# Cutting the last 512 output columns of an attention and mixture-of-experts kernel into three pieces in place of two

## The chip, the cores and the metric

The kernel runs on one core of one Trainium2 chip. The metric is the device time of one execution in microseconds (us); less is better. A core has five engines that run side by side and wait for each other through semaphores: TensorE (matmuls, PE in the profile, with its weight loads shown as PEld), VectorE (DVE), ScalarE (ACT), GpSimd (POOL) and SyncE (SP, which issues most of the DMA transfers here). Matmuls write to PSUM, a small memory from which VectorE or ScalarE take the results into SBUF, and DMA engines bring those to the chip's main memory.

## What is computed

Two stages. Multi-query attention on a batch of 8, with 16 heads, 384 positions and a head size of 64 gives 3072 rows of 1024 numbers. Then each row goes to one of 16 experts (4 groups of 4), the one that two gates choose:

```python
# attention, per head: attn = softmax(q k^T / 8) ; x = attn v, rows of 16*64
for g in range(G):                       # 4 groups
    ...
    for e in range(Eg):                  # 4 experts in a group
        h = np.maximum(xg[mask_e] @ w1[g, e], 0.0)
        ye = h @ w2[g, e]
        out[tok_idx] = (g_w * e_w)[:, None] * ye     # cut: selection of rows
```

w1 and w2 are 1024 x 1024 for each expert. Nearly all rows of one batch element choose the same expert, and the kernel is built on that: for each batch element it computes the whole 384 rows with the expert chosen most often, weighs each row by its gate (zero for rows that chose another expert), and then adds the few remaining rows of one further batch element and expert in a compact form. Anything beyond that is done in a conditional block that normally isn't entered.

## The kernel before

The second product of each batch element is done in units: `st` is one of three blocks of 128 rows, `nh` one of two halves of 512 columns. `side` takes one of three PSUM buffers in turn. `P` is 128, `CW` 512, `FO` 8.

```python
def y_unit(st, nh):
    for i in range(parts(st, nh)):
        n = CW // parts(st, nh)
        cs = slice(nh * CW + i * n, nh * CW + (i + 1) * n)
        y = place(st, cs)
        ps = side([P, n], FP32, "yps")
        for fo in range(FO):
            nc.tensor.matmul(out=ps[:], lhsT=state["h"][:, fo, st * P:(st + 1) * P],   # L417
                             rhs=w2[:, fo, cs], start=(fo == 0), stop=(fo == FO - 1))
        if merge is None or not merge(st, cs, ps, y):
            nc.scalar.activation(out=y, in_=ps[:], func=ACTF.Copy, scale=gs_of()[:, st:st + 1])
        store(st, cs, y)
```

The closing unit is the second half (`nh == 1`) of the last row block of the last batch element. It is the last one to run. There, the remaining rows are merged in: `spread` puts them in their places with four small matmuls into two PSUM buffers (`lo` in a buffer of its own, `lo2` in one of the three), VectorE adds the first half to the row that is ready, and ScalarE copies the second half to SBUF (`yl`). Each piece of the closing unit is then scaled by the gate and added to its part of `yl` in one VectorE operation, and stored with a transfer of its own.

```python
def store(st, cs, y):
    if closes(st):
        if cs.start == 0:
            leftover["row"] = y
        else:
            nc.sync.dma_start(out=outv[b, :, st, cs], in_=y)                 # L445
    elif cs.stop == Dm:
        nc.sync.dma_start(out=outv[b, :, st, :], in_=rows[st][:])            # L447

def merge(st, cs, ps, y):
    if not closes(st) or cs.start == 0:
        return False
    if cs.start == CW:
        spread()
    nc.vector.scalar_tensor_tensor(out=y, in0=ps[:], scalar=gsel[b][:, st:st + 1],      # L454
        in1=leftover["y"][:, cs.start - CW:cs.stop - CW], op0=OP.mult, op1=OP.add)
    return True
# the closing unit has two parts, every other unit one:
return moe_units(..., lambda st, nh: 2 if closes(st) and nh == 1 else 1)

def spread():
    lo = [ps_m.tile([P, 2, CW], FP32, tag="o", name="lo"), side([P, 2, CW], FP32, "lo2")]
    for i in range(2):
        for c in (i, 2 + i):
            nc.tensor.matmul(out=lo[c // 2][:, c % 2, 0:QW], ...)            # L463
    row = leftover["row"]
    nc.vector.tensor_add(out=row..., in0=row..., in1=lo[0][:, :, 0:QW])      # L465
    nc.sync.dma_start(out=outv[B - 1, :, ST - 1, 0:CW], in_=row)             # L466
    t = pool.tile([P, CW], FP32, tag="pt", bufs=9, name="yl")
    nc.scalar.copy(out=t[:]..., in_=lo[1][:, :, 0:QW])                       # L468
    leftover["y"] = t
```

After the closing unit comes the condition of the rare block. Every engine loads the flag `rarei` from SBUF and branches on it:

```python
fill(1)                                            # runs the closing unit
nc.vector.tensor_scalar(out=raref[:, 0:1], ...)    # L754
nc.vector.tensor_scalar(out=raref[:, 1:2], ...)    # L755
nc.vector.tensor_add(out=rarei[:], in0=raref[:, 0:1], in1=raref[:, 1:2])     # L757
rare = nc.values_load(rarei[0:1, 0:1], ...)        # L758
# cut: functions used in the block only
rare_block = tc.If(rare > 0, preferred_fallthrough_block=False)              # its end is L810
with rare_block:
    ...                                            # a long block, not entered here
```

Of the kernel before, what the change touches and what calls it, by code (L numbers as in the profile page):

```python
# [13 lines left out]
P = 128  # L14
# [7 lines left out]
def kernel(  # L22
# [25 lines left out]
    CW = 512  # L48
# [27 lines left out]
    def side(shape, dtype, name):  # L76
        return ps_s.tile(shape, dtype, tag="s", name=name)

    q_raw, k_raw, v_sb, kT, qT, pt, xT, xbf, gsel, wts = {}, {}, {}, {}, {}, {}, {}, {}, {}, {}
# [315 lines left out]
        nc.vector.reduce_sum(out=gs[:], in_=gm[:], axis=AX)  # L395
        gsel[b] = gs

    def moe_units(w1, w2, xb, gs_of, place, store, merge=None, parts=lambda st, nh: 1):
        units = []
        state = {}  # L400

        def h_unit(fc):
            if fc == 0:
                state["h"] = pool.tile([P, FO, S], BF16, tag="hT", bufs=1, name="hT")
            ps = side([P, CW], FP32, "hps")
            for ko in range(KO):
                nc.tensor.matmul(out=ps[:, 0:S], lhsT=w1[:, ko, fc * P:(fc + 1) * P], rhs=xb[:, ko, :], start=(ko == 0), stop=(ko == KO - 1))  # L407
            nc.scalar.activation(out=state["h"][:, fc, :], in_=ps[:, 0:S], func=ACTF.Relu)  # L408

        def y_unit(st, nh):  # L410
            for i in range(parts(st, nh)):
                n = CW // parts(st, nh)
                cs = slice(nh * CW + i * n, nh * CW + (i + 1) * n)
                y = place(st, cs)
                ps = side([P, n], FP32, "yps")
                for fo in range(FO):
                    nc.tensor.matmul(out=ps[:], lhsT=state["h"][:, fo, st * P:(st + 1) * P], rhs=w2[:, fo, cs], start=(fo == 0), stop=(fo == FO - 1))  # L417
# [4 lines that stand above are left out]
        for fc in range(FO):  # L422
            units.append(lambda fc=fc: h_unit(fc))
        for st in range(ST):
            for nh in range(2):
                units.append(lambda st=st, nh=nh: y_unit(st, nh))
        return units

    def first_units(b):
        rows = {}  # L430

        def place(st, cs):
            if cs.start == 0:
                rows[st] = pool.tile([P, Dm], FP32, tag="y", bufs=3, name="y")
            return rows[st][:, cs]

        def closes(st):
            return b == B - 1 and st == ST - 1
# [14 lines that stand above are left out]
                spread()  # L453
            nc.vector.scalar_tensor_tensor(out=y, in0=ps[:], scalar=gsel[b][:, st:st + 1], in1=leftover["y"][:, cs.start - CW:cs.stop - CW], op0=OP.mult, op1=OP.add)  # L454
            return True
        return moe_units(wts[b][0], wts[b][1], xbf[b], lambda: gsel[b], place, store, merge, lambda st, nh: 2 if closes(st) and nh == 1 else 1)

    def spread():
        lo = [ps_m.tile([P, 2, CW], FP32, tag="o", name="lo"), side([P, 2, CW], FP32, "lo2")]
        for i in range(2):  # L460
            for c in (i, 2 + i):
                r = slice(CAP * c, CAP * c + CAP)
                nc.tensor.matmul(out=lo[c // 2][:, c % 2, 0:QW], lhsT=leftover["spread"][r, :], rhs=leftover["yc"][r, :], start=True, stop=True, tile_position=(CAP * c, 0))  # L463
        row = leftover["row"]
        nc.vector.tensor_add(out=row.rearrange("p (c n) -> p c n", c=2), in0=row.rearrange("p (c n) -> p c n", c=2), in1=lo[0][:, :, 0:QW])  # L465
        nc.sync.dma_start(out=outv[B - 1, :, ST - 1, 0:CW], in_=row)  # L466
        t = pool.tile([P, CW], FP32, tag="pt", bufs=9, name="yl")
        nc.scalar.copy(out=t[:].rearrange("p (c n) -> p c n", c=2), in_=lo[1][:, :, 0:QW])  # L468
        leftover["y"] = t
# [13 lines left out]
    def fill(n):  # L483
        while n > 0:
            if not units:
                if begun[0] >= B or begun[0] not in wts:
                    return
                units.extend(first_units(begun[0]))
                begun[0] += 1
            units.pop(0)()  # L490
            n -= 1
            ran[0] += 1
            if ran[0] == (FO + 2 * ST) * (B - 2) + FO:
                leftover_w1()
            if ran[0] == (FO + 2 * ST) * (B - 1):
                leftover_w2()
# [87 lines left out]
    for p in range(NP):  # L584
        b, st = divmod(p, ST)
# [49 lines left out]
        if p in PHASES:  # L635
            n = PHASES[p]
# [135 lines left out]
    def pair_units(b_reg, w1, w2, xe, ge):  # L772
        acc = pool.tile([P, ST, Dm], FP32, tag="xT", bufs=1, name="acc")

        def store(st, cs, y):
            if st == ST - 1 and cs.stop == Dm:
                nc.gpsimd.dma_start(out=outv[bass.ds(b_reg, 1)].rearrange("a p s d -> (a p) s d"), in_=acc[:], accum_op=OP.add, max_dma_last_dim=4096)
        return moe_units(w1, w2, xe, lambda: ge, lambda st, cs: acc[:, st, cs], store)
# [31 lines left out]
    with rare_block:  # L810
# [7 lines left out]
      with tc.If(ok < 1):  # L818
# [4 lines left out]
          with tc.For_i(0, B * H, 1) as i:  # L823
# [13 lines left out]
              for qt in range(ST):  # L837
# [5 lines left out]
                  at = pool.tile([P, S], FP32, tag="presum", bufs=1, name="at")  # L843
# [62 lines left out]
```

## Time and profile before

| | before |
|---|---|
| time, median of three runs | 460.92 us (460.87 to 461.02) |
| span of the profiled execution | 459.6 us |
| TensorE busy | 449.4 us, 98% |
| VectorE busy | 308.4 us, 67% |
| ScalarE busy | 242.0 us, 53% |
| closing unit, first piece's matmuls begin | 449.66 us |
| last compute operation (L757) begins | 453.08 us |

The span is the time from the first to the last instruction of one profiled execution. Times in the timeline and in the chain of work are counted from its start. In a line of the timeline stand the start, the duration, the engine, the line of the kernel and the operation with its output and inputs; in brackets, idle time of the engine ahead of it and what ended it. "x8" says that eight instructions are merged in the line. A name with a q (SPq, PEldq) is the instruction queue of an engine: waits, branches, register loads and the issue of transfers, which don't count as work.

### The profile page before, as it was taken

The page shows a single profiled execution, that of the slowest core. Times are in us where ns is not written, and L with a number is a line of the kernel's source. Part 1 is how long each engine was busy: PE and PEld are TensorE (multiplying, and loading weights), DVE is VectorE, ACT ScalarE, POOL GpSimd, SP SyncE. Part 2 cuts the span into 40 slices and gives each one's busy share as a digit, 9 for nine tenths or more (in the row PEclk, how much of TensorE's full clock was granted, in tenths as well). Part 3 has the DMA queues.
Part 4 walks back from the last instruction along what each step waited for, and adds up shares of the span by engine and source line. Part 5 has one row for each costly group of instructions (what it writes and reads, how often), then busy time and mean ns, then how long its engine had stood idle before and what let it go on. Part 6 is the DMA issues. An engine that isn't in the chain of part 4 may idle for free.

```text
span 459.6 us, 10200 instructions
## 1 busy us (share of the span) xinstructions
PE 449.4 (98%) x4208; PEld 199.8 (43%) x4208; DVE 308.4 (67%) x488; ACT 242.0 (53%) x345; POOL 60.5 (13%) x83
## 2 busy tenths in 40 slices
PE   8999999999999999999999999999999999999893
PEld 6343445333643345433553335433454335434552
DVE  3899965499717996099843997269960999574411
ACT  2966643676337753576346773376535764542331
POOL 1004003000120113000030001200130000500000
PEclk9999999999999999999999999999999999999997
DMA  8787997996699395992979747994869910799982
GB/s 154 99 146 109 218 208 120 258 201 139 107 177 254 74 189 96 235 224 74 157 113 266 140 118 124 167 258 80 170 102 233 234 69 11 115 211 245 274 212 104
DMA packets 152454, 74.55 MB, mean 162 GB/s; under 512 B 120256, under 2 KB 138944, under 8 KB 152400
## 3 DMA queue, kind: packets, MB, share of 16 engines
q0 software_dynamic: 28416, 37.81, 48.4%
q1 hardware_dynamic: 122656, 35.68, 33.3%
q8 instruction: 35, 0.57, 0.5%
q10 hardware_dynamic: 1328, 0.33, 0.4%
q14 instruction: 19, 0.16, 0.1%
HBM read 92.62 MB, written 19.01 MB: 243 GB/s over the span
## 4 chain that ended last, share of the span: by engine, by line
PE 89%; DMA 4%; issue 2%; DVE 1%; POOL 0%; ACT 0%; ACTq 0%; SPq 0%; POOLq 0%
PE s L251 28%; PE o L290 25%; PE hps L407 16%; PE yps L417 16%; PE gps L312 2%; DMA x_bf<-xbf 2%; DMA xe<-x_bf 2%; DMA qn<-in_q_dram 1%; PE qps L228 1%; POOL xbf L301 0%; DVE presum L261 0%; PE sm L273 0%; PE pb L715 0%; DVE rinv L280 0%; DVE xT L300 0%
## 5 line engine op out<-in xcount | busy, mean ns | idle before, releaser
L253 ACT ACTIVATE pt<-s 128x1024 f32<-128x1024 f32 x144 | 142.1, 1026 | 72.3 <-PE s L251 71.5
L251 PE MATMUL s<-qT,kT 64*64 64x512 f32 x1152 | 142.7, 594 | 0.0
L290 PE MATMUL o<-pt,v 64*64 64x512 f32 x1152 | 141.1, 590 | 0.0
L261 DVE TENSOR_TENSOR presum<-presum,pt 128x1024 f32<-128x1024 f32 x96 | 116.6, 1215 | 15.2 <-ACT pt L253 9.8
L407 PE MATMUL hps<-xbf,w 128*128 128x384 bf16 x512 | 86.7, 326 | 0.0
L417 PE MATMUL yps<-w,hT 128*128 128x512 bf16 (+1 forms) x392 | 85.7, 375 | 0.0
L259 DVE TENSOR_TENSOR presum<-pt 128x1024 f32<-128x1024 f32 x24 | 29.4, 1223 | 76.8 <-ACT pt L253 75.4
L290 PEld LDWEIGHTS o<-pt,v 64*64 64x64 f32 x1152 | 43.4, 133 | 76.8 <-issue 73.0
L251 PEld LDWEIGHTS s<-qT,kT 64*64 64x64 f32 x1152 | 40.8, 133 | 66.8 <-issue 60.0
L301 POOL CAST xbf<-xT 128x1024 bf16<-128x1024 f32 x24 | 25.0, 1043 | 302.8 <-DVE xT L300 302.8
L407 PEld LDWEIGHTS <-w 128*128 128x128 bf16 x512 | 48.2, 98 | 37.6 <-issue 6.5
L419 ACT ACTIVATE y<-yps,gsel 128x512 f32<-128x512 f32 x47 | 32.3, 688 | 58.8 <-PE yps L417 57.2
L408 ACT ACTIVATE hT<-hps 128x384 bf16<-128x384 f32 x64 | 31.3, 489 | 52.1 <-PE hps L407 48.0
L417 PEld LDWEIGHTS <-hT 128*128 128x128 bf16 x392 | 37.6, 98 | 44.1 <-issue 2.4
L145 POOL DMA_DIRECT2D w<-in_moe_w_dram x36 | 24.8, 708 | 58.2 <-DVE gsel L395 45.0
L300 DVE TENSOR_TENSOR xT<-o,rinv 128x1024 f32<-128x1024 f32 x24 | 29.2, 1215 | 2.5 <-PE o L290 2.5
L280 DVE STREAM_TRANSPOSE rinv<-rc 128x1024 f32<-128x1024 f32 x24 | 29.9, 1246 | 0.8
L265 DVE TRANSPOSE_TENSOR_REDUCE fold<-presum 128x32 f32<-128x1024 f32 x24 | 29.6, 1232 | 0.0
L243 DVE STREAM_TRANSPOSE qT<-qraw 128x1024 f32<-128x1024 f32 x20 | 23.6, 1202 | 0.0
L209 ACT ACTIVATE qraw<-qraw 128x1024 f32<-128x1024 f32 x21 | 22.0, 1048 | 0.0
L273 PEld LDWEIGHTS sm<-fold,sel 64*64 64x64 f32 x192 | 7.3, 133 | 13.3 <-issue 13.3
L371 ACT ACTIVATE ex<-dl 128x60 f32<-128x60 f32 x8 | 2.0, 253 | 20.1 <-DVE dl L369 20.1
(152 smaller groups left out, 162.0 us busy)
## 6 DMA issues: line engine op xcount, KB each, us to landing
w<-in_moe_w_dram POOLq DMA_DIRECT2D x36, 512.0 KB, 11.5
w<-in_moe_w_dram POOLq DMA_DIRECT2D x9, 2048.0 KB, 26.0
out_dram<-y SPq DMA_DIRECT2D x23, 512.0 KB, 6.9
qraw<-in_q_dram SPq DMA_DIRECT2D x56, 192.0 KB, 3.7
x_bf<-xbf SPq DMA_DIRECT2D x8, 768.0 KB, 3.9
v<-in_v_dram SPq DMA_DIRECT2D x16, 96.0 KB, 3.1
k<-in_k_dram SPq DMA_DIRECT2D x28, 48.0 KB, 2.7
qn<-in_q_dram SPq DMA_DIRECT2D x4, 256.0 KB, 5.2
```

The costliest lines, as they stand in the source:

```text
L251: nc.tensor.matmul(out=ps[64 * c:64 * c + 64, a, :], lhsT=kT[b][r, j * D:(j + 1) * D], rhs=qT[p][r, c * CW:(c + 1) * CW], start=True, stop ...
L253: nc.scalar.activation(out=t[:], in_=ps[:], func=ACTF.Exp, scale=scale)
L259: nc.vector.tensor_add(out=presum[p][:], in0=pt[p, 0][:], in1=pt[p, 1][:])
L261: nc.vector.tensor_add(out=presum[p][:], in0=presum[p][:], in1=pt[p, j][:])
L265: nc.vector.tensor_reduce(out=fold[p][:], in_=presum[p][:].rearrange("p a (n i) -> p (a n) i", i=32), axis=AX, op=OP.add, apply_transpose= ...
L280: nc.vector.transpose(out=t[:].rearrange("p (b i) -> p b i", i=32), in_=rc[:].rearrange("p c b -> p (c b)").unsqueeze(2).to_broadcast([P, ...
L290: nc.tensor.matmul(out=o_ps[p][64 * a:64 * a + 64, c, :], lhsT=v_sb[b][r, j, :], rhs=pt[p, j][r, a, :], start=(j == 0), stop=(j == KB - 1))
L300: nc.vector.tensor_mul(out=xT[b][:, :, ts], in0=o_ps[p][:].rearrange("p c (h n) -> p (c h) n", n=P), in1=rinv[p][:].rearrange("p (h n) -> ...
L407: nc.tensor.matmul(out=ps[:, 0:S], lhsT=w1[:, ko, fc * P:(fc + 1) * P], rhs=xb[:, ko, :], start=(ko == 0), stop=(ko == KO - 1))
L408: nc.scalar.activation(out=state["h"][:, fc, :], in_=ps[:, 0:S], func=ACTF.Relu)
L417: nc.tensor.matmul(out=ps[:], lhsT=state["h"][:, fo, st * P:(st + 1) * P], rhs=w2[:, fo, cs], start=(fo == 0), stop=(fo == FO - 1))
L419: nc.scalar.activation(out=y, in_=ps[:], func=ACTF.Copy, scale=gs_of()[:, st:st + 1])
```

## The change

The closing unit's 512 columns are computed, merged and stored in pieces of 256, 128 and 128 columns, where there were two of 256. It is meant to leave less to do once the last matmul is through: a smaller last merge and a smaller last store. All other units stay in one piece of 512.

```diff
-    def moe_units(w1, w2, xb, gs_of, place, store, merge=None, parts=lambda st, nh: 1):
+    def moe_units(w1, w2, xb, gs_of, place, store, merge=None, parts=lambda st, nh: (4,)):
...
         def y_unit(st, nh):
-            for i in range(parts(st, nh)):
-                n = CW // parts(st, nh)
-                cs = slice(nh * CW + i * n, nh * CW + (i + 1) * n)
+            at = nh * CW
+            for part in parts(st, nh):
+                n = part * P
+                cs = slice(at, at + n)
+                at += n
                 y = place(st, cs)
                 ps = side([P, n], FP32, "yps")
...
-        return moe_units(wts[b][0], wts[b][1], xbf[b], lambda: gsel[b], place, store, merge, lambda st, nh: 2 if closes(st) and nh == 1 else 1)
+        return moe_units(wts[b][0], wts[b][1], xbf[b], lambda: gsel[b], place, store, merge, lambda st, nh: (2, 1, 1) if closes(st) and nh == 1 else (4,))
```

## The prediction, made before the changed kernel was run

> **What bounds the kernel now.** I read the page first, for where the whole time goes; then the chain of work that ended last, for the stretch in which the change lies; then the timeline of the last ten microseconds; then the records of the lines after it, because the chain stops well ahead of the end of the span.
>
> ```profile
> span 459.6 us, 10200 instructions
> PE 449.4 (98%) x4208; PEld 199.8 (43%) x4208; DVE 308.4 (67%) x488; ACT 242.0 (53%) x345; POOL 60.5 (13%) x83
> ```
>
> TensorE is the bound of the body. The change touches only what comes after 449.6 us, so 98% of the span stays as it is instruction for instruction, and the question is what sets the last ten microseconds.
>
> ```profile
> 449.72 0.98 PE yps L417 x8
> 450.70 0.71 PE lo L463 x8
> 451.42 0.04 issue
> 451.46 0.69 DVE y L465
> 452.14 0.80 DVE y L454 x2
> 452.94 0.05 DVE raref L754
> 452.98 0.07 DVE raref L755
> 453.06 0.02 issue
> 453.08 0.15 DVE rarei L757
> ```
>
> This is the end of the chain (start, us, what). TensorE is in it up to the first closing piece and the four spreading products. After 451.46 us it is VectorE without a gap: the row sum, the two merges (L454), the three tiny operations that make the flag `rarei`. The second piece's matmuls are not in the chain: they run beside the row sum.
>
> ```profile
> 450.63 0.71 PE L463 MATMUL lo<-yc,of_last 32*128 32x256 f32 x8
> 451.28 1.05 PE L417 MATMUL yps<-w,hT 128*128 128x256 bf16 x8
> 451.44 0.59 ACT L468 COPY yl<-lo 128x512 f32<-128x512 f32 x1 [1.19 <-PE lo L463]
> 452.06 0.48 DVE L454 SCALAR_TENSOR_TENSOR y<-yps,gsel,yl 128x256 f32<-128x256 f32 x1
> 452.46 0.48 DVE L454 SCALAR_TENSOR_TENSOR y<-yps,gsel,yl 128x256 f32<-128x256 f32 x1
> 452.85 0.13 DVE L754 TENSOR_SCALAR raref<-small 1x1 f32<-1x1 f32 x1
> 452.93 0.83 SPq L445 DMA_DIRECT2D out_dram<-y  x2
> ```
>
> From start to start the merges are 0.40 and 0.39 us apart. The second one could have begun at 452.33 (when its matmuls end), but began at 452.46, when VectorE had room: VectorE is the bound there by 0.13 us. The chain stops at 453.23 us, and the span at 459.6. What lies between is the conditional block on `rarei`:
>
> ```profile
> L758 PEldq TENSOR_LOAD <-rarei x1: 967/967/967, 453.3 to 453.3; - x1
> L810 PEldq COMPARE_BRANCH  x2: 95/1986/3876, 454.3 to 454.8; - x2
> L810 SPq COMPARE_BRANCH  x2: 38/46/53, 454.5 to 456.1; - x2
> L901 PEldq DRAIN  x2: 7/40/73, 458.7 to 459.1; - x2
> L901 ACTq DRAIN  x2: 8/44/80, 457.0 to 459.1; - x2
> L901 DVEq DRAIN  x2: 10/34/57, 457.6 to 459.1; - x2
> L901 SPq DRAIN  x3: 7/7/13, 457.3 to 459.1; - x3
> ```
>
> Each engine loads `rarei` and branches over the block. TensorE's second branch starts at 454.8 and takes 3.876 us, so TensorE reaches its first drain at 458.7; ScalarE is there at 457.0, SyncE at 457.3, VectorE at 457.6. The barrier that ends the program waits for the last of them. So the end is rarei (453.23), plus the load, plus TensorE's branch. SyncE waits for the output stores to land in this stretch, and still arrives 1.4 us before TensorE. The stores do not set the end.
>
> **What the Trainium skill says.** "Runtime: NRT & Kernel Launch", section Instruction fetch mechanics: a taken branch whose target lies outside the fetched pages stalls until the target page has been brought in by DMA. The trace agrees: 3.876 us on TensorE against 0.095 us for its other branch. "VectorE: DVE Perf Modes", section The TRN2 errata: an operation from PSUM to SBUF takes 120 cycles plus one per element at 0.96 GHz. For 256 elements that is 392 ns; the trace has 400 and 392 ns from start to start. For 128 it gives an estimate of 248 cycles, 258 ns. "TensorE: Matmul & The Clock Gate", section Back-to-back issue gap, gives two spacings for a 128-column matmul, about 56 ns for a single isolated one and about 81 ns in a stream with weight loads. The trace decides for the first: the 24 transposes of L715, with a weight load each, are 1.8 us busy in three groups of 8, thus 0.6 us a group, and with 219 ns for the last one 0.38/7 = 54 ns of spacing. "DMA: Bandwidth & Descriptors", section Anatomy of one DMA: about 2.0 us of fixed cost[...], so a half-sized store is not a half-time store. The trace has 2.5 us to landing for a 128 KB piece.
>
> **The change part by part.** The order of the built program shows these edits and nothing else on the working path: eight 256-column matmuls become sixteen of 128 columns (with eight more weight loads), one 256-wide merge becomes two of 128, one 128 KB store becomes two of 64 KB. Two waits matter: the matmuls of piece two wait for something long past, those of piece three wait for ScalarE. That is the copy L468, which empties the PSUM buffer of `lo2`; the pool has three buffers, and piece three gets that one.
>
> TensorE: piece two begins at 451.28 as now, and takes 7 x 0.055 + 0.22 = 0.60 us, to 451.88. Piece three needs the buffer of `lo2`: the copy ends at 451.44 + 0.59 = 452.03. With some 0.05 us to get going (VectorE's first merge waits for the same copy and starts 0.03 us after it) it runs from 452.08 to 452.68. Now the last matmul ends at 452.33; TensorE is done 0.35 us later.
>
> VectorE: the first merge stays at 452.06 and holds the engine to 452.46. Piece two is ready (451.88), so its merge runs from 452.46 to 452.72. Piece three is ready at 452.68, plus some 0.03 us of signal 452.71, so its merge starts at about 452.73 and ends its hold at 452.73 + 0.26 = 452.99. L754 begins at 452.99 and not at 452.85: 0.14 us later. In other words, 256 elements cost the same, but the fixed 120 cycles (125 ns) are paid once more, and the wait for piece three adds about 0.01.
>
> From there, `rarei`, the five loads and TensorE's branch each move by 0.14 us, with nothing beside them to hide it: 459.6 becomes about 459.75 us.
>
> SyncE: issues are about 0.4 us each (the first of two starts at 452.93, the second some 0.4 later, together 0.83). The third issue adds 0.4 to 0.8 us with its extra wait ahead of it, and the last landing moves from about 453.3 + 2.5 = 455.8 to some 456.3 or 456.6. SyncE then reaches its drain at 457.8 to 458.1. TensorE is at 458.7 + 0.14 = 458.85. That is still hidden, by some 0.7 us.
>
> One small cost more: the third store moves its 64 KB at about 455 us, close to the time at which TensorE's page is fetched by the same DMA engines. I put 0.04 us on it, a choice and not a measurement. Sum: 460.92 + 0.14 + 0.04 = 461.1 us.
>
> **The rivals.** First, what the change is for: a shorter last piece leaves less to do after the last matmul (0.26 us of merge in place of 0.39). If matmuls set the end, 0.13 us would be gained, 460.8 us. Against it: VectorE has no gap from 451.46 on, and piece three has to wait for the copy. Second, the stores set the end: then the last landing counts, later by 0.4 to 0.8 us less about 0.15 for the halved bytes (an estimate from that DMA section's 436 GB/s), 461.2 to 461.6 us. Against it: SyncE's 1.4 us of slack at its drain. For it: that slack shrinks by half. Third, the PSUM buffer: had piece three got the buffer of piece one, it would wait until the first merge ends at 452.54, finish at about 453.2, and delay the flag by 0.6 us, 461.6 us. Against it: the wait is on ScalarE and not on VectorE. Fourth, the place of TensorE's code: sixteen more instructions move the branch's target against the fetched pages. If a page more or less has to be fetched, 3.876 us changes by some tenths or more, either way. Nothing in the profile speaks for it, and I give it about one in ten.
>
> **Range and chances.** Three runs of before lie within 0.15 us, so a tenth is visible. My path gives 461.1; the first rival is the low side, the second the high side, and the fetch can go both ways. 460.8 to 461.5 should hold it 8 times in 10. Two per cent are 9.2 us, more than the whole stretch from the first closing piece to the end's barrier could lose or gain by such an edit: 0.005 for faster, 0.99 for within, 0.005 for slower.
>
> **What would show it.** Right: VectorE shows three merges of about 0.48, 0.35 and 0.35 us (the overhang of 0.08 beyond the hold stays), 0.40 and 0.26 us apart, L754 at about 453.0; piece three starts just after L468 ends; TensorE's long branch is again near 3.9 us and its drain last; SyncE's drain before 458.3. Wrong: L754 at 452.85 or earlier (first rival); SyncE's drain last (second); piece three starting after 452.5 (third); TensorE's branch changed by over 0.2 us (fourth), which would carry the total out of my sum whatever VectorE does.

## The result, and the profile after

| | before | changed |
|---|---|---|
| time, median of six runs | 460.99 us | 462.91 us |
| ratio to before | | 1.0038, 95% interval 1.0025 to 1.0051 |
| span of the profiled execution | 459.6 us | 459.6 us |
| time less span | 1.6 us (that execution) | 2.6 to 3.3 us (six runs), median 3.1 |

The changed kernel is slower by 0.38%, about 1.75 us (1.92 us between the two medians), where 0.18 us was forecast. The span in the profile did not grow. The last row was worked out from each run's time and span, and is where the loss shows: **it lies outside the stretch from the first to the last recorded instruction.**

First the part inside, the end of the chain of work (start, us, what), which answers to the chain shown of before:

```profile
449.61 0.98 PE yps L419 x8
450.59 0.71 PE lo L465 x8
451.30 0.04 issue
451.34 0.69 DVE y L467
452.03 0.93 DVE y L456 x3
452.96 0.05 DVE raref L756
453.01 0.07 DVE raref L757
453.08 0.02 issue
453.10 0.15 DVE rarei L759
```

All of this stretch begins 0.11 us earlier in this execution; lengths are to be compared, not starts. The merges now take 0.93 us of the chain in place of 0.80. The timeline of the same kernel, third piece and merges:

```profile
451.33 0.58 ACT L470 COPY yl<-lo 128x512 f32<-128x512 f32 x1 [1.19 <-PE lo L465]
451.96 0.61 PE L419 MATMUL yps<-w,hT 128*128 128x128 bf16 x8 [0.18 <-ACT yl L470]
451.95 0.48 DVE L456 SCALAR_TENSOR_TENSOR y<-yps,gsel,yl 128x256 f32<-128x256 f32 x1
452.35 0.61 DVE L456 SCALAR_TENSOR_TENSOR y<-yps,gsel,yl 128x128 f32<-128x128 f32 x2
452.61 0.35 DVE L456 SCALAR_TENSOR_TENSOR y<-yps,gsel,yl 128x128 f32<-128x128 f32 x1
452.88 0.13 DVE L756 TENSOR_SCALAR raref<-small 1x1 f32<-1x1 f32 x1
```

The third piece waits 0.18 us for ScalarE's copy and takes 0.61 us. The merges start at 451.95, 452.35 and 452.61, then the flag's first operation at 452.88: 0.40, 0.26 and 0.27 us. From the first merge to the flag's first operation it is 0.93 us, and was 0.79. And the records of the conditional block and of the end:

```profile
L812 PEldq COMPARE_BRANCH  x2: 95/1988/3882, 454.3 to 454.8; - x2
...
L903 SPq DRAIN  x3: 7/7/13, 457.0 to 459.1; - x3
...
L903 PEldq DRAIN  x2: 8/40/73, 458.7 to 459.1; - x2
```

TensorE's long branch takes 3.882 us (3.876 before), its drain is again at 458.7, SyncE's at 457.0. Nothing here costs 1.75 us. What does differ is the record of TensorE's granted clock past the end of the span. Stretches of half a microsecond follow; the last three columns are the clock, the DMA share and GB/s. Before:

```profile
461.50:462.00 0.50, 0.00 (x0) 0.00 (x0) 0.00 (x0) 0.00 (x0) 0.00 (x0) 0.78 0.00 0
462.00:462.50 0.50, 0.00 (x0) 0.00 (x0) 0.00 (x0) 0.00 (x0) 0.00 (x0) 1.00 0.00 0
```

After:

```profile
461.50:462.00 0.50, 0.00 (x0) 0.00 (x0) 0.00 (x0) 0.00 (x0) 0.00 (x0) 0.50 0.00 0
...
462.50:463.00 0.50, 0.00 (x0) 0.00 (x0) 0.00 (x0) 0.00 (x0) 0.00 (x0) 0.54 0.00 0
```

A record of half the clock, which covers the end of the span, lasts to about 461.7 us before (0.78 is 44% of that stretch at 0.5) and to about 462.95 after (92% of its stretch). Both spans end at 459.6. What this mark stands for is not shown, but it moved by 1.25 us, and in the same two executions the time less the span grew from 1.6 to 2.8 us. So the loss was to be sought after the last recorded instruction, in something that the change does to it. The built program gives a candidate: TensorE has 4680 instructions in place of 4665, VectorE 865 in place of 864, SyncE 441 in place of 439.

### The profile page after: what moved, and what is told of

Its sections match the earlier page's. It is cut to its first block, busy times and chain, and to the rows that moved or that the text cites. A ratio compares the mean times of both kernels' runs of the same rounds, so it can differ in the third digit from the quotient of the medians.

```text
span 459.6 us, 10219 instructions
## 1 busy us (share of the span) xinstructions
PE 449.6 (98%) x4216; PEld 200.1 (44%) x4216; DVE 308.4 (67%) x489; ACT 241.9 (53%) x345; POOL 60.3 (13%) x83
## 4 chain that ended last, share of the span: by engine, by line
PE 89%; DMA 4%; issue 2%; DVE 1%; POOL 0%; ACT 0%; ACTq 0%; SPq 0%; POOLq 0%
PE s L251 28%; PE o L290 25%; PE hps L407 16%; PE yps L419 16%; PE gps L312 2%; DMA x_bf<-xbf 2%; DMA xe<-x_bf 2%; DMA qn<-in_q_dram 1%; PE qps L228 1%; POOL xbf L301 0%; DVE presum L261 0%; PE sm L273 0%; PE pb L717 0%; DVE rinv L280 0%; DVE xT L300 0%
## 5 line engine op out<-in xcount | busy, mean ns | idle before, releaser
L419 PE MATMUL yps<-w,hT 128*128 128x512 bf16 (+2 forms) x400 | 85.9, 371 | 0.2 <-ACT yl L470 0.2
```

## The experiments

**Which part of the change costs it.** Three runs add instructions to the kernel before, inside the rare block, which is never entered; so they are in the program and are not executed. The fourth is the changed kernel with its last two pieces stored in one transfer.

```diff
 def list_rest():
+    pz = side([P, CW], FP32, "pz")                     # e1: TensorE, N = 8, sixteen instructions
+    for _ in range(N):
+        nc.tensor.matmul(out=pz[:, 0:P], lhsT=ones_bf[:], rhs=ones_bf[:], start=True, stop=True)
```
```diff
+    dz = pool.tile([P, 1], FP32, tag="fl", bufs=1, name="dz")      # e2: VectorE, one instruction
+    nc.vector.memset(dz[:], 0.0)
```
```diff
+    sz = pool.tile([P, 128], FP32, tag="pt", bufs=9, name="sz")    # e3: SyncE, two instructions
+    nc.sync.dma_start(out=sz[:], in_=out[0:P, 0:128])
```
```diff
-                    nc.sync.dma_start(out=outv[b, :, st, cs], in_=y)       # e4, in the changed kernel
+                    lo = cs.start if cs.stop < Dm else cs.start - P
+                    if cs.stop != Dm - P:
+                        nc.sync.dma_start(out=outv[b, :, st, lo:cs.stop], in_=rows[st][:, lo:cs.stop])
```

> The kernel before, with eight 128-column matmuls and their eight weight loads added inside the rare block, which is never entered: sixteen more TensorE instructions in the program, none of them executed. Theory (the extra 1.9 us lie ahead of the first instruction, where two more 8 KB instruction fetches are seen, and come from the place of some engine's code): if TensorE's code is the one, 462.3 to 463.0 us at a span of 459.6, and fetches from about -10.5 us on. Rival A (the extra time is paid for executed work, in the closing pieces): 460.9 to 461.1. Rival B (it is the code of VectorE or SyncE): 460.9 to 461.1 as well.

> The kernel before, with one memset on VectorE added inside the never entered rare block: VectorE's program is one instruction longer, as the changed kernel's is (865). If VectorE's code makes the start later: 462.3 to 463.0 us. If TensorE's or SyncE's code does, or executed work: 460.9 to 461.1.

> The kernel before, with one transfer of 64 KB on SyncE's queue added inside the never entered rare block: SyncE's program is two instructions longer, as the changed kernel's is (441). If SyncE's code makes the start later: 462.3 to 463.0 us. If TensorE's or VectorE's code does, or executed work: 460.9 to 461.1.

> The changed kernel (pieces of 256, 128, 128), but its last two pieces are stored in one transfer of 128 KB: two stores as before. TensorE's and VectorE's programs are those of the changed kernel, SyncE's has 439 instructions as before. If the third store or SyncE's code is the cause: 460.9 to 461.3 us. If TensorE's or VectorE's code is: 462.3 to 463.0. By the steps of the prediction alone, about 461.1.

| run | time us | ratio to before (95%) | time less span, median (range) |
|---|---|---|---|
| before, beside these | 460.86 | | 1.53 (1.45 to 1.63) |
| e1, TensorE +16, not executed | 462.62 | 1.0033 (1.0022 to 1.0045) | 2.88 (2.59 to 3.32) |
| e2, VectorE +1 | 461.00 | 1.0002 (0.9994 to 1.0010) | 1.53 (1.46 to 1.60) |
| e3, SyncE +2 | 460.78 | 1.0003 (0.9995 to 1.0011) | 1.54 (1.46 to 1.62) |
| e4, changed, two stores | 462.56 | 1.0037 (1.0024 to 1.0050) | 2.93 (2.78 to 3.18) |

Sixteen TensorE instructions that never run cost what the change costs. Two stores in place of three don't take the loss away, and one instruction more on VectorE or two on SyncE don't make it. One part of the theory stated with e1 fell: more instruction fetches ahead of the first instruction are in the traces of e2 and e3 as well (13 and 14 packets in the last 12 us ahead of it, 13 in the changed kernel, 11 in the kernel before), and e2 and e3 are as fast as before. The loss is not at the start.

**Is it the length or the place?** Now fewer TensorE instructions in the changed kernel (e5), and more in the kernel before (e6 with N = 128, e7 with N = 64, both with the edit of e1).

```diff
-            for ko in range(KO):                        # e5, in the changed kernel
-                nc.tensor.matmul(..., stop=(ko == KO - 1))
+            kos = KO - 4 if merge is None and fc == 0 else KO      # merge is None in the rare block only
+            for ko in range(kos):
+                nc.tensor.matmul(..., stop=(ko == kos - 1))
```

> The changed kernel, with sixteen TensorE instructions taken out of the rare block, which is never entered (it leaves out four of the eight products of one of its units, in its two copies): TensorE's program has 4664 instructions, one fewer than before. All executed work is that of the changed kernel. If the place of TensorE's code costs the time: back near before, at 460.9 + 0.15 to 0.3 = 461.0 to 461.2 us, and 1.5 to 1.6 us between time and span instead of some 3. If the executed pieces cost it: 462.5 to 463.0.

> The kernel before with 256 TensorE instructions added inside the never entered block, 16 KB of code if an instruction has 64 bytes: a whole number of the 16 KB fetches that the trace shows for TensorE. If it matters where TensorE's last instructions lie in such a page: 460.7 to 461.2 us, as before. If a longer program is simply slower: 462.6 us or more.

> As the last, with 128 instructions, half a page. If the slow case is a stretch of the page that the last instructions and what the runtime adds after them just reach over: 460.7 to 461.2 us when that stretch is shorter than 128 instructions, 462.3 to 463.0 when it is longer. If a longer program is simply slower: 462.6 or more.

The changed kernel with 4664 TensorE instructions took 461.08 us beside 460.83 of before, ratio 1.0006 (1.0000 to 1.0013), with 1.53 us between time and span. 256 and 128 more instructions in the kernel before gave 461.26 and 460.83 us, ratios 1.0006 (0.9998 to 1.0014) and 1.0000 (0.9992 to 1.0008), with 1.55 and 1.50 us. So a longer program is not slower. It is the place.

**Where the slow stretch lies.** The edit of e1 again, with N = 2 (e9), 32 (e10), 48 (e11), 16 (e15) and 5 (e16); and the changed kernel with N = 32 (e13) and N = 128 (e14).

> The kernel before with four TensorE instructions (two matmuls, two weight loads) added inside the never entered block. It tells how near the kernel before stands to the slow stretch, which has begun by sixteen. Theory (a 16 KB page boundary that comes to lie inside what TensorE still has to run after the last recorded instruction): either 460.9 us with 1.5 us between time and span, or some 462.5 with 2.6 to 3.3 us; nothing between. A cost that grows with each instruction would give 461.3.

> The kernel before with 64 TensorE instructions inside the never entered block. Sixteen were slow, 128 not. Theory: still slow (462.3 to 463.0, 2.6 to 3.3 us between time and span) if what runs after the last recorded instruction is longer than about 64 instructions; otherwise as before, 460.9 and 1.5. Should the boundary fall among TensorE's last recorded instructions, the span itself would be about 1.3 us longer and the difference to the time 1.5.

> As the last, with 96 instructions: it halves the stretch between 64 and 128 in which the slow case ends. Theory: slow (462.3 to 463.0) or as before (460.9), and slow only if 64 is slow too.

> The changed kernel, whole, with 64 more TensorE instructions inside the never entered block. If the place of TensorE's code alone makes the changed kernel slow, more code makes it fast again: 461.0 to 461.2 us, 1.5 us between time and span, as the run with sixteen instructions fewer. If more code costs more: 463 or more.

> The changed kernel with 256 more TensorE instructions inside the never entered block. If the slow stretch comes back with every 256 instructions: slow like the changed kernel, 462.3 to 463.0 us, with 2.6 to 3.3 us between time and span. If it was an accident of these few lengths: 461.1.

> The kernel before with 32 TensorE instructions inside the never entered block: between 16 (slow) and 64 (as before). Either 460.9 us with 1.5 us between time and span or 462.3 to 463.0 with 2.6 to 3.3; with the boundary among the last recorded instructions, a span longer by about 1.3 us.

> The kernel before with ten TensorE instructions inside the never entered block: between 4 (as before) and 16 (slow). Either 460.9 us with 1.5 us between time and span or 462.3 to 463.0 with 2.6 to 3.3.

| TensorE instructions more than before | run | ratio to before (95%) | time less span, median us |
|---|---|---|---|
| 4 | e9 | 0.9998 (0.9990 to 1.0006) | 1.52 |
| 10 | e16 | 1.0027 (1.0018 to 1.0037) | 2.87 |
| 32 | e15 | 0.9992 (0.9984 to 1.0001) | 1.53 |
| 64 | e10 | 0.9997 (0.9989 to 1.0006) | 1.53 |
| 96 | e11 | 0.9992 (0.9984 to 1.0000) | 1.53 |
| changed + 64 | e13 | 1.0002 (0.9994 to 1.0011) | 1.54 |
| changed + 256 | e14 | 1.0038 (1.0025 to 1.0052) | 3.04 |

The changed kernel, whole, is as fast as before when its TensorE program gets 64 more instructions that never run, and slow again with 256. The slow stretch begins between 4 and 10 more instructions and ends before 32. It comes back after 256, the one distance at which a slow length was tried again. That fits a page of 16 KB, the size of one TensorE fetch, at 64 bytes an instruction; these lengths alone would fit a period of 128 as well.

**The wait itself.** So far all that costs time lies where no record is. If TensorE waits there for its next page of code (one fetch of 16 KB), then at a length near the end of the slow stretch the page boundary moves in among the instructions that are recorded. N = 10 (e17) and N = 13 (e18) looked for it.

> The kernel before with 20 TensorE instructions inside the never entered block: between 16 (slow) and 32 (as before). If what stalls is the fetch of the next page within TensorE's last instructions, then close to the end of the slow stretch the boundary moves in among the instructions that the profile records: the span would grow by about 1.3 us, with TensorE's last drains late in it, and the difference between time and span fall back to 1.5. Otherwise 462.5 with 2.6 to 3.3 between them, or 460.9 with 1.5.

> As the last with 26 instructions. The same three outcomes; one of the two may hit the few lengths at which the stall would be seen inside the span.

With 20 it is still outside: 462.19 us, ratio 1.0030 (1.0019 to 1.0040), 2.87 us between time and span. With 26 it is inside: 463.20 us, ratio 1.0043 (1.0027 to 1.0060); the spans of its runs are 461.5 to 462.0 us, beside a mean of 459.5 of before, so they grew by 2.3 us and not by the 1.3 of the forecast, and the difference to the time has fallen to 1.34 us. The records of the last line of e18 (durations min/median/max in ns, first and last start):

```profile
L904 PEldq DRAIN  x2: 8/40/73, 458.2 to 458.6; - x2
L904 ACTq EVENT_SEMAPHORE  x2: 17/17/17, 458.4 to 459.0; - x2
L904 DVEq EVENT_SEMAPHORE  x2: 21/21/21, 458.4 to 459.0; - x2
L904 PEldq EVENT_SEMAPHORE  x2: 51/51/51, 458.4 to 461.7; - x2
```

ScalarE and VectorE take their last semaphore at 459.0 us; TensorE takes its own at 461.7, 2.7 us later, with nothing left to wait for from them. Its drain just ahead was at 458.6. The DMA record from 458.5 us on shows what was under way (40 slices of 1.5 us in all; queue, packets, MB, share of 16 engines):

```profile
GB/s 0 0 0 0 0 0 0 437 0 0 0 0 0 0 0 0 0 0 0 0 0 0 0 0 0 0 0 0 0 0 0 0 0 0 0 0 0 0 0 0
...
q8 instruction: 1, 0.02, 5.5%
```

One instruction fetch of 0.02 MB begins at about 458.8 and takes 5.5% of 16 x 1.5 us = 1.3 us, to 460.1. It is the only transfer. TensorE goes on after it, but not at once: 1.6 us later. (That the 16 KB fetches of queue q8 are TensorE's is inferred from the one ahead of it, which lies inside TensorE's long branch.)

The kernel before has the same fetch; here from 459 us on, in slices as above:

```profile
GB/s 0 0 0 0 0 0 0 0 437 0 0 0 0 0 0 0 0 0 0 0 0 0 0 0 0 0 0 0 0 0 0 0 0 0 0 0 0 0 0 0
...
q8 instruction: 1, 0.02, 3.6%
```

It begins at 459.3, 0.7 us after the end of TensorE's long branch, and is under way when the span ends at 459.6. All 20 traces have this fetch, 0.7 to 1.2 us after the branch. So the slow lengths add no fetch; at 26 instructions more, TensorE needs the page while it is still on its way. The 1.6 us after the transfer have their like in the branch itself: in the kernel before its fetch runs from 455.80 to 457.13, and the branch ends at 458.67, 1.5 us later (1.4 to 1.7 in the 20 traces).

**Does the flag set the end of the span?** Two runs on the kernel before: the three operations of the flag moved ahead of the closing unit (e8), and besides the first piece's store issued by ScalarE's queue (e12).

```diff
-    fill(1)
-    assert ran[0] == UNITS * B
     raref = ...                                         # e8: the flag's lines stay as they are
     nc.vector.tensor_add(out=rarei[:], ...)
+    fill(1)
+    assert ran[0] == UNITS * B
```
```diff
-                    nc.sync.dma_start(out=outv[b, :, st, cs], in_=y)      # e12, with the edit of e8
+                    (nc.scalar if cs.start == CW else nc.sync).dma_start(out=outv[b, :, st, cs], in_=y)
```

> The kernel before, with the three small VectorE operations that make the flag moved ahead of the closing unit; nothing else. If the flag and TensorE's branch set the end: TensorE can load the flag as soon as its own matmuls are through (452.2 in place of 453.27), and the whole moves by about 1.0 us, to 459.9. If the stores or SyncE set the end: 460.9 as before.

> The kernel before with the flag made ahead of the closing unit (as in the run that moved it alone), and with the first piece's store issued by ScalarE's queue, which is idle there, in place of SyncE's. If the landings of the stores took over as the end once the flag was early: the stores are issued 0.4 us earlier, and 460.0 to 460.5 us. If the stores land later because they share the DMA engines with the instruction fetches, and not because they are issued late: 460.9 to 461.3, as with the flag alone.

Neither gained: 461.32 us, ratio 1.0007 (0.9999 to 1.0015), and 461.09 us, ratio 1.0003 (0.9995 to 1.0011). So the 459.9 us forecast for e8, should the flag and TensorE's branch set the end, did not come. In the trace of e8 the flag did what it was to do, and something else took its place:

```profile
L810 PEldq COMPARE_BRANCH  x2: 95/2186/4276, 451.2 to 452.6; - x2
...
L901 SPq DRAIN  x3: 7/7/13, 458.4 to 458.7; - x3
...
L901 PEldq DRAIN  x2: 8/40/73, 456.9 to 458.8; - x2
...
DMA to landing us min/median/max: 3.6/3.7/3.7
```

TensorE's branch starts at 452.6 in place of 454.8, and TensorE drains at 456.9. But SyncE, which waits for the stores, drains at 458.4 in place of 457.3, because the two stores land 3.6 to 3.7 us after their issue, and took 2.5 before (the last line is of their record, L445). Issued 0.3 us earlier still in e12, they took 3.8 and 3.9 us, so a late issue is not the reason. The page for TensorE's branch is fetched earlier in both, among the stores: in e8 from 454.05 to 455.28 us, and 23 packets of the stores, at about 24 GB/s, come only after 455.3. In the kernel before, that fetch begins at 455.80 and no packet of a store comes after 455.3. That the fetch held these packets up is inferred: the records don't say which DMA engine carried them. In the kernel before, then, the flag and TensorE's branch do come last, but taking a microsecond off them gains nothing, because the stores take their place.

## Why the prediction was wrong

The range of 460.8 to 461.5 us missed 462.9. By its steps:

- *TensorE's pieces:* right. Third piece 0.05 us after the copy, 0.61 us long (forecast 0.05 and 0.60), its products 55 to 56 ns apart.
- *VectorE's merges:* right. 0.48, 0.34 and 0.35 us, apart by 0.40, 0.26 and 0.27; the flag 0.14 us later from the first merge on, as forecast.
- *TensorE's branch:* right, 3.882 us beside 3.876. That it agrees to 6 ns is luck: in the traces of the other runs with the flag at its old place it takes 3.52 to 4.06 us. So the 0.04 us that I put on the fetch meeting the third store could not have been seen; in this trace the last store packet ends at 455.1, ahead of the fetch at 455.7.
- *SyncE:* wrong, without effect. I forecast its drain at 457.8 to 458.1, it came at 457.0. The three stores landed 1.8 to 2.4 us after issue and not 2.5, so the third issue was made up for. The 2.0 us of fixed cost that the prediction takes from the Trainium skill, "DMA: Bandwidth & Descriptors", section Anatomy of one DMA, are given there for transfers issued by GpSimd; these are SyncE's, and the measured landings decide.
- *The whole:* where TensorE's code is the right length, the changed kernel costs 1.0006 (e5) and 1.0002 (e13) of before, 0.28 and 0.09 us, neither clear of zero. The forecast 0.18 us lies between and is neither confirmed nor refuted. The prediction's "so a tenth is visible" was wrong: it rested on three runs within 0.15 us, and the 49 of the kernel before beside e5 lie between 460.23 and 461.74.
- *The step that failed* is the last one, "From there, `rarei`, the five loads and TensorE's branch each move by 0.14 us, with nothing beside them to hide it: 459.6 becomes about 459.75 us", and from it the sum 460.92 + 0.14 + 0.04. It adds a change of the span to a time that is 1.5 us longer than the span, and takes these 1.5 us as given. They became 2.6 to 3.3 us, because fifteen more TensorE instructions moved its last ones to another place in the pages of code.

The fourth rival had named the cause, the place of TensorE's code, but looked for it in the branch of 3.876 us, with a chance of one in ten. It was after the last recorded instruction.

What is shown: fifteen or sixteen TensorE instructions more, run or not, make the loss; at one fewer, four more, or 32, 64, 96, 128 and 256 more it is absent; the changed kernel loses it with 64 more and has it again with 256; and at 26 more a wait of 2.7 us at TensorE's last instructions is seen, over one fetch of code and 1.6 us after it. What is inferred: that the 1.2 to 1.75 us of the other slow lengths are the same wait, in instructions that run after the kernel's own. The trace has no record there. An estimate fits: the page under way at the end of the span has landed at 460.2 us in both kernels, and with the 1.6 us of e18 it can be used from 461.8. The profiled execution of the kernel before took 461.2 us and is over by then; that of the changed kernel took 462.4. (This counts the device time from the start of the span, which is not shown.) The Trainium skill, "Runtime: NRT & Kernel Launch", section Instruction fetch mechanics, fits both parts: code comes in blocks of 16 KB, 256 instructions, the next one is fetched while the current one runs, and a taken branch breaks that sequence. Its remark that the cost of a block boundary is mostly hidden does not hold here: TensorE's branch ends 0.5 us (e18, 458.1 to 458.6) to 0.9 us (before, 458.7 to 459.6) ahead of its last recorded instructions, and the next page's fetch begins only 0.7 us after the branch.

## What to carry to other kernels

Compare time less span ahead of any explanation: where it differs between two kernels, that part of the difference is not in the chain of work. This kernel, whose program ends behind a taken branch, lost more than 1 us to a few instructions on one engine, so test a small edit to a kernel of that kind at a second code length (instructions in a block that is not entered do) ahead of judging the edit itself. The split of the last piece bought nothing here, because the matmuls did not set the end: from the first merge to the flag VectorE needed 0.14 us more. That it pays where matmuls do set the end is not shown by any run.

## What the runs showed of the hardware that was not expected

- TensorE's code length decides 1.2 to 2 us of time at the end of this program: slow at 10, 15, 16, 20, 26 and 271 instructions more than before, as before at -1, 4, 32, 64, 79, 96, 128 and 256.
- After a fetch of 16 KB of TensorE's code has landed, 1.4 to 1.7 us pass until the instruction that waited for it is through: the long branch in all 20 traces, the last semaphore in e18 (1.6 us).
- Time less span is steady to within 0.2 us (1.45 to 1.63) in all runs of kernels outside that stretch. The half-clock record ends 2.0 to 2.1 us after the span in their traces, and 3.3 to 3.5 us after it in those of the slow kernels, e18 apart (1.9).
- A 128 KB store landed 2.5 us after issue in the kernel before and 3.7 us in e8, where the TensorE branch came 2.2 us earlier.
